# X by tokens through DRAM: VectorE turns squares and DMA reorders them, in place of TensorE's transposes

## Chip, cores and metric

One core of one Trainium2 chip runs the whole program. The metric is device microseconds of one execution, the median of several runs; lower is better.

## What is computed

Batch 4, 448 tokens, 12 heads of 64, so a model width of 768. An attention with sigmoid weights is followed by two token and channel blocks:

```python
x = sigmoid(q @ k.T / 8 - log(448)) @ v              # heads joined: (4, 448, 768)
u = x + (x.T @ U @ V).T                              # first block, tokens mixed at rank 32
x = u + relu(u @ w_ch1) @ w_ch2                      # 768 -> 3072 -> 768
theta = x @ w_theta                                  # second block: a rotation of x
zr, zi = x * cos(theta), x * sin(theta)
y = w_tok_r @ zr + w_tok_i @ zi                      # per batch, over tokens
u = x + y
out = u + relu(u @ w_ch)
```

## The kernel before

All of x stays on the chip as X, [128 partitions, 6, 1792]: feature d*128 + p on partition p of slab d, tokens of the four batches along the row. Nearly every product is done as three fp32r matmuls (high by high, high by low, low by high), so each operand is split in two parts, by ScalarE (high, `hi_act`) and by VectorE or GpSimd (low, `lo_dve`, `lo_pool`, lines 110 to 119).

The order of all instructions is written out by hand, engine by engine, in program order. The stages that matter here:

- **The channel block**, 12 blocks i of 256 hidden columns times 4 batches b. `ch1(i, b)` makes g in PSUM with 36 matmuls, ScalarE and VectorE split it (gh L671, gl L672), and `ch2(i, b)` runs a stage later: three tiles y (e2 = 0, 1, 2) of 12 matmuls each, from a ring of two PSUM buffers, each added to X by VectorE (L690). After each tile a function `after(e2)` does one or two steps of weight conversion (`tick`). So a y tile needs the buffer that the add of two tiles earlier frees. In the last block (i = 11, called L in the code) the order on TensorE is ch2(batch 0), ch1(batch 2), ch2(batch 1), ch1(batch 3), ch2(batch 2), ch2(batch 3).
- In that last block SyncE also loads tok (3.1 MB, the split token matrices) and three of the split w_theta slabs, and brings the last conversions in and out (`ws_wc`, `th_d`, `wc_d`).
- **The rotation**, 14 chunks of 128 tokens. `project(c)` makes theta for 128 tokens (36 matmuls, L799 to L803) in a ring of two PSUM tiles; `trig(c)` reduces it on VectorE (t1, L819 and L820, which frees the PSUM tile) and takes sine and cosine on ScalarE; `split_x(c + 2)` splits X for a later chunk; `zmake(c)` multiplies x by sine and cosine on VectorE (L854 and L856, or L864 and L865 for a chunk that lies in two batches) and splits the products (zh on ScalarE, zl mostly on GpSimd). Theta has tokens on partitions, X has features there, so `natural(c)` turns X first: six transposes of 128x128 on TensorE into PSUM (xn, L811). After chunks 4, 7 and 13 follow `mix(0)`, `mix(1)`, `mix(2)` and then `mix(3)`: six tiles of 21 matmuls each over the tokens of a batch, added to X by VectorE (L881) from two PSUM buffers. `zmake` of the chunk before stands inside `project(c)` on TensorE, after half of its matmuls, or inside a mix after its second tile.
- The tiles t1 and t2 come from rings of two, zr from a ring of two. A name in the profile is that of the tile, without its numbers.

All DMAs named here are issued by SyncE (SPq in the profile), one after another in program order, each when what it waits for has come.

Of the kernel before, what the change touches and what calls it, by code (L numbers as in the profile page):

```python
# [11 lines left out]
F32 = mybir.dt.float32  # L12
# [7 lines left out]
def f(t):  # L20
    return t.bitcast(F32)
# [3 lines left out]
def tile_kernel(  # L25
# [15 lines left out]
    nc = tc.nc  # L41
    B, H, S, D = q.shape
    DM = H * D
    R = moe_U.shape[1]
    DF = moe_w_ch1.shape[1]
    P = 128
    CP = 112
    NC = S // CP
    NK = DM // P
    NT = B * S  # L50
# [4 lines left out]
    HN = DM // 2  # L55
    NTC = NT // P
    REM = S % P
    NFULL = S // P
# [24 lines left out]
    cpool = ctx.enter_context(tc.tile_pool(name="cpool", bufs=1))  # L83
    wpool = ctx.enter_context(tc.tile_pool(name="wpool", bufs=1))

    dpool = ctx.enter_context(tc.tile_pool(name="dpool", bufs=1, space=bass.MemoryType.DRAM))

    ident = cpool.tile([P, P], F32, name="ident")
    bias_s = cpool.tile([P, 1], F32, name="bias_s")
    half_pi = cpool.tile([P, 1], F32, name="half_pi")  # L90
    X = cpool.tile([P, NK, NT], F32, name="X")
# [9 lines left out]
    def pool(name, side="left", space=None):  # L101
        st = ExitStack()
        kw = dict(name=name, bufs=1, side=side, reuse_waits="tile")
        if space is not None:
            kw["space"] = space
        return st.enter_context(tc.tile_pool(**kw)), st


    def hi_act(o, i):
        nc.scalar.activation(o, i, AF.Copy)  # L110
# [100 lines left out]

    kept = {}
    tok_d = dpool.tile([P, 2, NZ, S], F32, name="tok_d")

    def spill_tile(name):
        return late["sp"].tile([P, 2 * DM], F32, tag="sp", name=f"sp_{name}", bufs=1)
# [17 lines left out]
    def load_kept(name, tag):  # L234
        t = ring(tag, f"{name}_r")
        nc.sync.dma_start(out=f(t), in_=kept[name])
        return t
# [58 lines left out]
    late = {}  # L296
# [2 lines left out]
    ap, ap_st = pool("ap")  # L299
    ap1, ap1_st = pool("ap1")  # L300
    ap2, ap2_st = pool("ap2")
    ps_a, ps_a_st = pool("ps_a", "left", PSUM)
    ps_b, ps_b_st = pool("ps_b", "right", PSUM)
    u_in = ap.tile([P, 2, NS, R], F32, name="u_in")
# [167 lines left out]
    def U2(b, d, ps, hl, n=2):  # L472
        h, l = hl
        for m in range(n):
            nc.tensor.matmul(
                ps[:, m, :S], pc_t[b][:, (d + m) * P:(d + m + 1) * P], h, start=True, stop=False
            )
        for m in range(n):
            nc.tensor.matmul(
                ps[:, m, :S], pc_t[b][:2 * R, (d + m) * P:(d + m + 1) * P], l, start=False, stop=True  # L480
            )
        x = X[:, d:d + n, b * S:(b + 1) * S]
        nc.vector.tensor_add(x, ps[:, :n, :S], x)
# [28 lines left out]
    L = NB - 1  # L512
# [40 lines left out]
    def tick(i, b, t):  # L553
        for name in units.get((i, b, t), ()):
            plan[name].step()
# [26 lines left out]
    def split_u(b, p, d0, d1, *los):  # L582
        if d0 == 0:
            uh_t[b] = p.tile([P, NK, S], F32R, name=f"uh{b}")
            ul_t[b] = p.tile([P, NK, S], F32R, name=f"ul{b}")
        for d in range(d0, d1):
            x = X[:, d, b * S:(b + 1) * S]
            hi_act(uh_t[b][:, d], x)
            los[d % len(los)](ul_t[b][:, d], x, uh_t[b][:, d])
# [8 lines left out]
    for p in range(NP):  # L598
# [19 lines left out]
        b, r = divmod(p - 2 - NH, NH)  # L618
# [3 lines left out]
        b, r = divmod(p - 3 - NH, NH)  # L622
        if b >= 0 and r < NK // 2:
            ps = ps_a.tile([P, 2, 512], F32, tag="ux", name=f"h_{b}_{r}")
# [87 lines left out]

    u23, u23_st = pool("u23")
    ps_y, ps_y_st = pool("ps_y", "left", PSUM)
    def hook(i, b):
        def after(e2):
            if (i, b) == (0, 1):
                ps = ps_g.tile([P, FB, 512], F32, tag="g", name=f"hl_{e2}", bufs=2)
                U2(B - 1, 2 * e2, ps, (vhl, vll))
            if i == 0 and b in (1, 2):  # L720
                split_u(b + 1, u23, 2 * e2, 2 * e2 + 2, lo_pool)
            tick(i, b, e2 + 2)
        return after
# [15 lines left out]
    for i in range(NB):  # L739
        for b in range(B):  # L740
            tick(i, b, 0)
            if (i, b) not in ((0, 0), (0, 1)):
                ch1(i, b)
            if i == L and b == 1:
                u01_st.close()
                tokhl, tokhl_st = pool("tokhl", "right")
                ctx.enter_context(tokhl_st)
                tok = tokhl.tile([P, 2, NZ, S], F32R, name="tok")
                nc.sync.dma_start(out=f(tok), in_=tok_d)
                tok_h, tok_l = tok[:, 0], tok[:, 1]  # L750
                xr, xr_st = pool("xr", "right")
                ctx.enter_context(xr_st)
            if i == L and b >= 2:
                split_x(b - 2)
            if i == L and b == 0:
                th_t[0] = load_kept("th0", "w1")
            if i == L and b == B - 1:
                th_t[2] = load_kept("th2", "w1")
                th_t[3] = load_kept("th3", "w1")
            if i == L and b == 1:  # L760
                th_t[1] = load_kept("th1", "w2")
            tick(i, b, 1)
            if prev is not None:
                ch2(*prev, hook(i, b))
            prev = (i, b)
            if (i, b) == (0, 1):
                uv_st.close()
                late["sp"], sp_st = pool("sp")
# [2 lines left out]
    th_t[4] = load_kept("th4", "w2")  # L771
    th_t[5] = load_kept("th5", "w2")
    sp_st.close()
    u23_st.close()
    gpool_st.close()
    cv_st.close()
# [6 lines left out]
    ps_e, st = pool("ps_e", "left", PSUM)  # L783
    ctx.enter_context(st)
    zp, st = pool("zp")
# [3 lines left out]
    def project(c, w, name, k0=0, k1=NK):  # L789

        if k0 == 0:
            pj_t[c] = ps_t.tile([P, 2, 512], F32, tag="th", name=f"{name}_{c}", bufs=2)
        ps = pj_t[c]
        h, l = xs_t[c]
        for kk in range(k0, k1):
            wh, wl = w[kk][:, 0], w[kk][:, 1]
            for j in range(2):
                sl = slice(j * HN, (j + 1) * HN)
                nc.tensor.matmul(ps[:, j, :HN], h[:, kk, :], wh[:, sl], start=kk == 0, stop=False)  # L799
                nc.tensor.matmul(ps[:, j, :HN], h[:, kk, :], wl[:, sl], start=False, stop=False)  # L800
            for j in range(2):
                sl = slice(j * HN, (j + 1) * HN)
                nc.tensor.matmul(ps[:, j, :HN], l[:, kk, :], wh[:, sl], start=False, stop=kk == NK - 1)  # L803
        return ps[:, :, :HN]

    def natural(c, name):

        ps = ps_e.tile([P, 2, 512], F32, tag="xn", name=f"{name}_{c}")
        for kk in range(NK):
            j, o = divmod(kk * P, HN)  # L810
            nc.tensor.transpose(ps[:, j, o:o + P], X[:, kk, c * P:(c + 1) * P], ident)  # L811
        return ps[:, :, :HN]

    def trig(c):

# [10 lines left out]
    def zsplit(key, t, lo):  # L826
        h = zp.tile([P, 2, HN], F32R, tag="zh", name=f"zh_{key[0]}_{key[1]}", bufs=12)
        l = zp.tile([P, 2, HN], F32R, tag="zl", name=f"zl_{key[0]}_{key[1]}", bufs=12)
        hi_act(h, t)
        lo(l, t, h)  # L830
        z_t[key] = (h.rearrange("p a n -> p (a n)"), l.rearrange("p a n -> p (a n)"))

    def where(c):
        pr, ci = divmod(c, 2 * NFULL + 1)
        return pr, ci, 2 * pr + (ci > NFULL), ci if ci < NFULL else ci - NFULL - 1

    def zmul(c):
        cos, sin = T_t[c]
        xn = natural(c, "xn")
        nc.vector.tensor_mul(sin, xn, sin)  # L840
        nc.vector.tensor_mul(cos, xn, cos)

# [6 lines left out]
    def zmake(c):  # L849
        pr, ci, b, i = where(c)  # L850
        if ci != NFULL:
            cos, sin = T_t.pop(c)
            xn = natural(c, "xn")
            nc.vector.tensor_mul(sin, xn, sin)  # L854
            zsplit((b, NFULL + i), sin, lo_pool)
            nc.vector.tensor_mul(cos, xn, cos)  # L856
            zsplit((b, i), cos, lo_pool)
        else:
            cos, sin = T_t.pop(c)
            xn = natural(c, "xn")  # L860
            for n in range(2):
                t = zp.tile([P, 2, HN], F32, tag="zr", name=f"zr_{c}_{n}", bufs=2)
                sl = slice(n * REM, (n + 1) * REM)
                nc.vector.tensor_mul(t[REM:], xn[sl], sin[sl])  # L864
                nc.vector.tensor_mul(t[:REM], xn[sl], cos[sl])  # L865
                zsplit((2 * pr + n, 2 * NFULL), t, lo_pool if n else lo_dve)

    def mix(b, after=None):
        for d in range(NK):
# [12 lines left out]
            if after is not None:  # L882
                after(d)

    project(0, th_t, "th", 0, 4)
    project(1, th_t, "th", 0, 4)
    for c in range(NTC):
# [52 lines left out]
    for bi, b in enumerate(turns_):  # L940
        for e2 in range(NK // 2):
# [3 lines left out]
            else:  # L945
                ps = ps_t.tile([P, 2, 512], F32, tag="th", name=f"wc_{b}_{e2}", bufs=2)
# [3 lines left out]
            for e in range(2):  # L950
                m = 2 * e2 + e
                o = ps1[e][:, 0, :S] if final else ps[:, e, :S]
# [42 lines left out]
```

## Time and profile before

| | us |
|---|---|
| median of 3 runs (lowest, highest) | 1170.18 (1169.7, 1170.59) |
| the profiled execution | 1170.08 |
| its span, first to last instruction | 1168.3 |
| TensorE matmuls busy | 1155.3 |
| VectorE, ScalarE, GpSimd busy | 647.9, 360.9, 189.5 |
| last block of the channel block, ch2(batch 0) to the end of ch2(batch 3) | 830.9 to 875.2 |
| rotation, first project to the start of mix(3) | 875.2 to about 1053 |

The first two lines are times of whole executions; the rest is read from the trace of one of them, in us from its first instruction. A matmul's end is modelled and overlaps the next one, so a row's duration is longer than the step from one start to the next; that step is what a chain is made of. On VectorE, too, the next instruction starts about 0.1 us before the one ahead is over.

### The profile page before, as it was taken

How to read it: one execution, taken by the hardware profiler on the slowest of the kernel's cores; microseconds unless marked ns; L12 is line 12 of the kernel's file. 1: busy time of each engine (PE TensorE's matmuls, PEld its weight loads, DVE VectorE, ACT ScalarE, POOL GpSimd, SP SyncE). 2: the span in 40 equal slices, each digit the busy share in tenths (PEclk: the TensorE clock that was granted, in tenths of full speed). 3: DMA queues.
4: the chain of work that ended last, by engine and by line, in shares of the span. 5: the costliest groups of instructions: out<-in, count | busy, mean ns of one | idle time of the engine just before them, and what ended most of it. 6: DMA issues, size and time to landing. Idle time of an engine off the chain costs nothing.

```text
span 1168.3 us, 15638 instructions
## 1 busy us (share of the span) xinstructions
PE 1155.3 (99%) x6414; PEld 1000.5 (86%) x6414; DVE 647.9 (55%) x805; ACT 360.9 (31%) x465; POOL 189.5 (16%) x136
## 2 busy tenths in 40 slices
PE   7999999999999999999999999999999999999998
PEld 3444458999999999999999999999999999999997
DVE  4777873445554555455545556565375542732443
ACT  5878872212221222122212222222125341630110
POOL 2300012211111111111111122222002321410000
PEclk9999999999999999999999999999999999999999
DMA  9887830113231323132313242424431000120444
GB/s 168 165 162 141 161 83 1 55 54 97 51 133 54 97 52 131 54 97 53 130 54 98 66 140 61 155 61 156 164 138 52 1 1 1 45 119 1 61 64 66
DMA packets 183719, 100.57 MB, mean 86 GB/s; under 512 B 151232, under 2 KB 174656, under 8 KB 183520
## 3 DMA queue, kind: packets, MB, share of 16 engines
q1 hardware_dynamic: 156800, 87.95, 28.3%
q0 software_dynamic: 2368, 8.24, 2.5%
q10 hardware_dynamic: 24480, 3.39, 2.0%
q8 instruction: 50, 0.82, 0.3%
q14 instruction: 21, 0.17, 0.0%
HBM read 81.40 MB, written 18.15 MB: 85 GB/s over the span
## 4 chain that ended last, share of the span: by engine, by line
PE 97%; DMA 1%; SPq 1%; DVE 1%; ACT 0%; issue 0%; ACTq 0%
PE g L664 10%; PE g L666 10%; PE g L665 10%; PE y L686 10%; PE y L688 10%; PE y L687 10%; PE av L419 5%; PE sc L393 4%; PE y L877 3%; PE y L876 3%; PE y L878 3%; PE th L799 3%; PE th L803 3%; PE th L800 2%; PE wc L958 2%; PE wc L959 2%
## 5 line engine op out<-in xcount | busy, mean ns | idle before, releaser
L690 DVE TENSOR_TENSOR X<-y,X 128x896 f32<-128x896 f32 x144 | 157.1, 1091 | 114.9 <-PE y L688 113.5
L686 PE MATMUL y<-gh,w 128*128 128x448 f32 x576 | 210.7, 366 | 0.2 <-DVE X L690 0.2
L664 PE MATMUL g<-uh,w 128*128 128x448 f32 x576 | 210.7, 366 | 0.0
L687 PE MATMUL y<-gl,w 128*128 128x448 f32 x576 | 210.4, 365 | 0.0
L688 PE MATMUL y<-gh,w 128*128 128x448 f32 x576 | 210.4, 365 | 0.0
L666 PE MATMUL g<-uh,w 128*128 128x448 f32 x576 | 210.4, 365 | 0.0
L665 PE MATMUL g<-ul,w 128*128 128x448 f32 x576 | 210.4, 365 | 0.0
L671 ACT ACTIVATE gh<-g 128x896 fp32r<-128x896 f32 x48 | 44.1, 919 | 390.8 <-PE g L666 390.8
L672 DVE SCALAR_TENSOR_TENSOR gl<-g,gh 128x896 fp32r<-128x896 f32 x48 | 52.4, 1092 | 183.8 <-ACT gh L671 183.8
L113 POOL TENSOR_TENSOR w<-ca_w,w 128x768 fp32r<-128x768 f32 x42 | 77.8, 1853 | 432.0 <-ACT w L110 432.0
L664 PEld LDWEIGHTS g<-uh,w 128*128 128x128 f32 x576 | 108.2, 188 | 9.8 <-ACT uh L110 0.7
L686 PEld LDWEIGHTS y<-gh,w 128*128 128x128 f32 x576 | 108.2, 188 | 9.7 <-issue 1.1
L688 PEld LDWEIGHTS y<-gh,w 128*128 128x128 f32 x576 | 108.2, 188 | 8.6
L666 PEld LDWEIGHTS g<-uh,w 128*128 128x128 f32 x576 | 108.2, 188 | 8.6
L687 PEld LDWEIGHTS y<-gl,w 128*128 128x128 f32 x576 | 108.2, 188 | 8.6
L665 PEld LDWEIGHTS g<-ul,w 128*128 128x128 f32 x576 | 108.2, 188 | 8.5
L384 ACT ACTIVATE A<-sc,bias_s 128x896 f32<-128x896 f32 x72 | 72.2, 1006 | 23.4 <-PE sc L393 12.8
L419 PE MATMUL av<-A,v 128*64 128x448 f32 x288 | 65.2, 561 | 0.0
L876 PE MATMUL y<-tok,zh 128*128 128x448 f32 x168 | 61.7, 367 | 0.0
L877 PE MATMUL y<-tok,zh 128*128 128x448 f32 x168 | 61.5, 366 | 0.0
L113 POOL TENSOR_TENSOR zl<-t,zh 128x768 fp32r<-128x768 f32 x23 | 42.7, 1880 | 115.4 <-ACT zh L110 115.4
L878 PE MATMUL y<-tok,zl 128*128 128x448 f32 x168 | 61.4, 366 | 0.0
(139 smaller groups left out, 1634.6 us busy)
## 6 DMA issues: line engine op xcount, KB each, us to landing
ws_w<-in_moe_w_ch_dram SPq DMA_DIRECT2D x40, 768.0 KB, 4.4
ws_w<-in_moe_w_ch_dram POOLq DMA_DIRECT2D x8, 768.0 KB, 5.9
k<-in_k_dram SPq DMA_DIRECT2D x94, 56.0 KB, 2.7
q<-in_q_dram SPq DMA_DIRECT2D x93, 56.0 KB, 3.1
ws_th<-in_moe_w_theta_dram SPq DMA_DIRECT2D x6, 768.0 KB, 4.3
th_d<-sp_th SPq DMA_DIRECT2D x6, 768.0 KB, 4.1
ws_wc<-in_moe_w_ch_dram SPq DMA_DIRECT2D x6, 768.0 KB, 4.7
wc_d<-sp_wc SPq DMA_DIRECT2D x6, 768.0 KB, 4.5
```

The lines of the kernel that those rows point to most:

```text
L113: nc.gpsimd.tensor_sub(o, a, b)
L419: nc.tensor.matmul(ps[h * D:(h + 1) * D, :S], v_t[p // 2][:, 2 * (p % 2) + h, c, :], A_t[p, c][:, h, :], start=c == 0 and p % 2 == 0, stop ...
L664: nc.tensor.matmul(o, wh[:, sl], uh_t[b][:, kk, :], start=kk == 0, stop=False)
L665: nc.tensor.matmul(o, wh[:, sl], ul_t[b][:, kk, :], start=False, stop=False)
L666: nc.tensor.matmul(o, wl[:, sl], uh_t[b][:, kk, :], start=False, stop=kk == NK - 1)
L686: nc.tensor.matmul(o, wh[:, sl], gh[:, j, :], start=j == 0, stop=False)
L687: nc.tensor.matmul(o, wh[:, sl], gl[:, j, :], start=False, stop=False)
L688: nc.tensor.matmul(o, wl[:, sl], gh[:, j, :], start=False, stop=j == FB - 1)
L690: nc.vector.tensor_add(x, ps[:, :, :S], x)
L876: nc.tensor.matmul(o, zh[:, sl], tok_h[:, i, :], start=n == 0, stop=False)
L877: nc.tensor.matmul(o, zh[:, sl], tok_l[:, i, :], start=False, stop=False)
L878: nc.tensor.matmul(o, zl[:, sl], tok_h[:, i, :], start=False, stop=n == NZ - 1)
```

## The change

X by tokens is no longer made by TensorE. VectorE turns X in squares of 32x32 (one instruction for a slab of 448 tokens, `turn_x`), SyncE writes the turned slab to DRAM (x_d), and later reads a chunk back so that tokens lie on partitions (`load_xn`: four DMAs of 32 partitions by 24 pieces of 32 numbers, 128 bytes each). The turns of batches 0, 1 and 2 stand in `after` of the last block, two behind each add, through a ring of three staging tiles; those of batch 3 stand behind the channel block and use buffers of t1 and t2. xn is now a tile in SBUF, from the ring zr, which has three buffers instead of two. The tile `ident` moves to another pool; it is now only used by the first transposes of the program.

```diff
+    x_d = dpool.tile([DM, NT], F32, name="x_d")
...
+    def turn_x(b, d, t):
+        nc.vector.transpose(out=t, in_=X[:, d, b * S:(b + 1) * S])
+        nc.sync.dma_start(out=x_d[d * P:(d + 1) * P, b * S:(b + 1) * S], in_=t)
+
     def hook(i, b):
         def after(e2):
+            if i == L and 0 < b < B:
+                for d in (2 * e2, 2 * e2 + 1):
+                    turn_x(b - 1, d, late["stg"].tile([P, S], F32, tag="stg", name=f"stg_{b}_{d}", bufs=3))
...
-    def natural(c, name):
-
-        ps = ps_e.tile([P, 2, 512], F32, tag="xn", name=f"{name}_{c}")
-        for kk in range(NK):
-            j, o = divmod(kk * P, HN)
-            nc.tensor.transpose(ps[:, j, o:o + P], X[:, kk, c * P:(c + 1) * P], ident)
-        return ps[:, :, :HN]
+    xn_t = {}
+
+    def load_xn(c):
+        t = xn_t[c] = zp.tile([P, 2, HN], F32, tag="zr", name=f"xn_{c}", bufs=3)
+        for a in range(P // R):
+            o = c * P + a * R
+            nc.sync.dma_start(
+                out=t[a * R:(a + 1) * R].rearrange("i a (g j) -> i (a g) j", j=R),
+                in_=x_d[:, o:o + R].rearrange("(g i) j -> i g j", i=R),
+            )
...
-            xn = natural(c, "xn")
+            xn = xn_t.pop(c)
...
+            load_xn(c + 1)
+        _, second, _, _ = where(c + 1)
+        if c + 2 < NTC and second != NFULL:
+            load_xn(c + 2)
...
+    load_xn(0)
+    load_xn(1)
+    for d in range(NK):
+        tag = f"t{d % 2 + 1}"
+        t = zp.tile([P, 2, HN], F32, tag=tag, name=f"stg_{B}_{d}", bufs=2).rearrange("p a n -> p (a n)")[:, :S]
+        turn_x(B - 1, d, t)
     project(0, th_t, "th", 0, 4)
     project(1, th_t, "th", 0, 4)
```

On VectorE, from the second add of batch 0 to the second add of batch 1 in the last block, there stood (L690 is the add of a y tile, L672 makes gl, L119 makes xl, the others convert w_theta; in brackets what an instruction waits for, DMAHW being a DMA's landing):

```order
L690 TENSOR_TENSOR X<-y_0_1_6653,X 128x2x448 [waits PE_49]
L151 SCALAR_TENSOR_TENSOR ws_th_6389<-ca_th_6636,ws_th_6389 128x768 [waits DVE_49,Activation_49]
L690 TENSOR_TENSOR X<-y_0_2_6668,X 128x2x448 [waits PE_49]
L157 SCALAR_TENSOR_TENSOR ca_th_6636<-ca_th_6636,ws_th_6389 128x768 [waits DVE_49,Pool_49]
L672 SCALAR_TENSOR_TENSOR gl_2_6721<-g_2_6683,gh_2_6720 128x896 [waits Activation_49]
L119 TENSOR_TENSOR xl_0_6725<-X,xh_0_6724 128x768 [waits Activation_49]
L690 TENSOR_TENSOR X<-y_1_0_6730,X 128x2x448 [waits PE_49]
```

and the same place of the changed kernel (lines are one higher or lower there; stg is a staging tile, L717 its turn):

```order
L691 TENSOR_TENSOR X<-y_0_1_6663,X 128x2x448 [waits PE_49]
L717 STREAM_TRANSPOSE stg_2_6677<-X 128x448 [waits DVE_49]
L717 STREAM_TRANSPOSE stg_3_6680<-X 128x448 [waits DMAHW5_49]
L150 SCALAR_TENSOR_TENSOR ws_th_6390<-ca_th_6640,ws_th_6390 128x768 [waits Activation_49]
L691 TENSOR_TENSOR X<-y_0_2_6684,X 128x2x448 [waits PE_49]
L717 STREAM_TRANSPOSE stg_4_6698<-X 128x448 [waits DMAHW6_49,DVE_49]
L717 STREAM_TRANSPOSE stg_5_6701<-X 128x448 [waits DMAHW7_49]
L156 SCALAR_TENSOR_TENSOR ca_th_6640<-ca_th_6640,ws_th_6390 128x768 [waits Pool_49]
L673 SCALAR_TENSOR_TENSOR gl_2_6743<-g_2_6705,gh_2_6742 128x896 [waits Activation_49]
L118 TENSOR_TENSOR xl_0_6747<-X,xh_0_6746 128x768 [waits Activation_49]
L691 TENSOR_TENSOR X<-y_1_0_6752,X 128x2x448 [waits PE_49]
```

Two turns now stand behind each add, and from the fourth on each waits for the landing of the write that frees its staging tile.

On SyncE, at the step from the channel block to the rotation, there stood the last spills, the last two loads of w_theta, and then only the loads of w_ch (wc), which come 140 us later:

```order
L231 DMA th_d<-sp_th_6846 128x1536 [waits DMAHW0_49,DVE_49,Activation_49]
L231 DMA wc_d<-sp_wc_6897 128x1536 [waits DMAHW1_49,Pool_49]
L236 DMA th_r<-th_d 128x1536 [waits DMAHW5_49,DMAHW2_49,PE_49]
L236 DMA th_r<-th_d 128x1536 [waits DMAHW3_49,DMAHW0_49,PE_49]
L236 DMA wc_r<-wc_d 128x1536 [waits DMAHW4_49,PE_49]
```

and now, behind the same two loads, the reads of chunks 0 and 1 and then the writes of batch 3:

```order
L236 DMA th_r<-th_d 128x1536 [waits DMAHW5_49,DMAHW0_49,PE_49]
L822 DMA xn_7008<-x_d 32x24x32 [waits DMAHW6_49]
L822 DMA xn_7008<-x_d 32x24x32 [waits DMAHW7_49]
L822 DMA xn_7008<-x_d 32x24x32
L822 DMA xn_7008<-x_d 32x24x32 [waits DMAHW1_49]
L822 DMA xn_7013<-x_d 32x24x32 [waits DMAHW2_49,DVE_49]
L822 DMA xn_7013<-x_d 32x24x32 [waits DMAHW3_49]
L822 DMA xn_7013<-x_d 32x24x32 [waits DMAHW4_49]
L822 DMA xn_7013<-x_d 32x24x32 [waits DMAHW5_49]
L718 DMA x_d<-stg_0_7018 128x448 [waits DMAHW6_49,DVE_49]
L718 DMA x_d<-stg_1_7021 128x448 [waits DMAHW7_49,DVE_49]
L718 DMA x_d<-stg_2_7024 128x448 [waits DMAHW0_49,DVE_49]
```

Eight reads stand between the loads of w_theta and the first write of batch 3; a DMA also waits for the landing of the eighth DMA ahead of it. On VectorE the fifth turn of batch 3 waits for the landing of that batch's first write, and the first instruction of trig(0) stands behind the sixth.

## Rows read from the trace of the kernel before

**Rows 1.** The page, busy time by engine.
```profile
PE 1155.3 (99%) x6414; PEld 1000.5 (86%) x6414; DVE 647.9 (55%) x805; ACT 360.9 (31%) x465; POOL 189.5 (16%) x136
```

**Rows 2.** Timeline of TensorE, five places: start us, us, what [idle before, releaser].
```profile
845.44 0.36 PE L686 MATMUL y<-gh,w 128*128 128x448 f32 x1
...
852.74 0.36 PE L664 MATMUL g<-uh,w 128*128 128x448 f32 x1
...
867.68 0.44 PE L686 MATMUL y<-gh,w 128*128 128x448 f32 x1 [0.20 <-DVE X L690]
...
875.20 0.34 PE L799 MATMUL th<-th_r,xh 128*128 128x384 f32 x1
...
918.17 0.81 PE L811 MATMUL xn<-ident,X 128*128 128x128 f32 x6
```

**Rows 3.** Timeline of VectorE in the last block.
```profile
854.67 0.95 DVE L157 SCALAR_TENSOR_TENSOR ca_th<-ca_th,ws_th 128x768 uint32<-128x768 uint32 x1
...
861.24 1.09 DVE L672 SCALAR_TENSOR_TENSOR gl<-g,gh 128x896 fp32r<-128x896 f32 x1 [5.63 <-ACT gh L671]
862.25 0.95 DVE L119 TENSOR_TENSOR xl<-X,xh 128x768 fp32r<-128x768 f32 x1
863.12 1.08 DVE L690 TENSOR_TENSOR X<-y,X 128x896 f32<-128x896 f32 x1
...
866.46 1.08 DVE L690 TENSOR_TENSOR X<-y,X 128x896 f32<-128x896 f32 x1
```

**Rows 4.** Timeline of VectorE at the start of the rotation.
```profile
885.80 0.96 DVE L819 TENSOR_SCALAR t<-th 128x768 f32<-128x768 f32 x1 [9.31 <-PE th L803]
...
895.94 0.96 DVE L854 TENSOR_TENSOR t<-xn,t 128x768 f32<-128x768 f32 x1 [2.00 <-PE xn L811]
...
900.16 2.52 DVE L119 TENSOR_TENSOR xl<-X,xh 128x768 fp32r<-128x768 f32 x1
...
917.50 0.61 DVE L881 TENSOR_TENSOR X<-y,X 128x448 f32<-128x448 f32 x1
```

**Rows 5.** The chain that ended last, 889 to 893 us: start, us, what.
```profile
891.04 0.35 PE th L803 x2
891.39 0.66 PE xn L811 x6
```

**Rows 6.** VectorE groups by form: busy us, mean ns of one, idle before.
```profile
L440 DVE STREAM_TRANSPOSE xT<-X 128x448 f32<-128x448 f32 x24 | 15.2, 637 | 0.1
```

**Rows 7.** Timeline of SyncE, two issues: start us, us of the issue.
```profile
831.97 0.35 SPq L194 DMA_DIRECT2D ws_wc<-in_moe_w_ch_dram  x1
...
873.20 0.32 SPq L231 DMA_DIRECT2D wc_d<-sp_wc  x1
```

**Rows 8.** DMA issues at 831.04, 831.97 and 875.4: KB, us from issue to landing.
```profile
tok<-tok_d SPq DMA_DIRECT2D x1, 3136.0 KB, 10.3
...
ws_wc<-in_moe_w_ch_dram SPq DMA_DIRECT2D x1, 768.0 KB, 13.1
...
th_r<-th_d SPq DMA_DIRECT2D x1, 768.0 KB, 5.7
```

**Rows 9.** Timeline of TensorE near 26 us.
```profile
26.16 0.59 PE L402 MATMUL sl<-qT,kT 64*64 64x448 f32 x2 [1.77 <-DVE qT L354]
```

**Rows 10.** Windows: stretch, busy us by engine (instructions), granted clock, DMA share, GB/s.
```profile
27.20:30.60 3.40, 3.40 (x14) 1.85 (x14) 3.07 (x7) 1.88 (x3) 0.55 (x2) 0.50 0.66 108
```

**Rows 11.** DMA queues, 1086 to 1092 us (pieces of 128 bytes): packets, MB, share.
```profile
q10 hardware_dynamic: 1503, 0.18, 22.8%
q1 hardware_dynamic: 1377, 0.17, 19.0%
```

**Rows 12.** DMA queues, 303 to 307.6 us (loads of 256-byte pieces).
```profile
q1 hardware_dynamic: 1856, 0.46, 44.5%
```

**Rows 13.** Timeline of GpSimd there.
```profile
894.61 7.25 POOL L113 TENSOR_TENSOR zl<-t,zh 128x768 fp32r<-128x768 f32 x4 [21.44 <-ACT zh L110]
```

More of the change, by code (lines that the diff above doesn't have):

```diff
@@ L86, in tile_kernel @@
     dpool = ctx.enter_context(tc.tile_pool(name="dpool", bufs=1, space=bass.MemoryType.DRAM))
-    ident = cpool.tile([P, P], F32, name="ident")
     bias_s = cpool.tile([P, 1], F32, name="bias_s")
@@ L301, in tile_kernel @@
     ap2, ap2_st = pool("ap2")
+    ident = ap2.tile([P, P], F32, name="ident")
     ps_a, ps_a_st = pool("ps_a", "left", PSUM)
@@ L752, in tile_kernel @@
                 ctx.enter_context(xr_st)
+                late["stg"], stg_st = pool("stg", "right")
             if i == L and b >= 2:
@@ L773, in tile_kernel @@
     sp_st.close()
+    stg_st.close()
     u23_st.close()
@@ L852, in zmake @@
             cos, sin = T_t.pop(c)
-            xn = natural(c, "xn")
+            xn = xn_t.pop(c)
             nc.vector.tensor_mul(sin, xn, sin)
@@ L859, in zmake @@
             cos, sin = T_t.pop(c)
-            xn = natural(c, "xn")
+            xn = xn_t.pop(c)
             for n in range(2):
-                t = zp.tile([P, 2, HN], F32, tag="zr", name=f"zr_{c}_{n}", bufs=2)
+                t = zp.tile([P, 2, HN], F32, tag="zr", name=f"zr_{c}_{n}", bufs=3)
                 sl = slice(n * REM, (n + 1) * REM)
```

## The prediction

> **What bounds the kernel now.** The page's busy times come first: TensorE is busy 1155.3 of 1168.3 us, the others at most 55% [rows 1]. The waits of TensorE say whether that is real: past the first 30 us it waits once, for 0.2 us, in the last block of the channel block, before the row at 867.68 [rows 2]. So a microsecond that leaves TensorE's stream is worth a microsecond, as long as no other engine is then late. Which one is near to late is read stage by stage. The timelines of VectorE show two places without room: the last tiles of the last block (an unbroken run from 861.24 to past 866.46, at whose end TensorE waits [rows 2, 3]) and the start of the rotation. There VectorE works from 885.80 to the first add of mix(0) at 917.50 [rows 4], and that add ends at 918.11, 0.06 us before TensorE has finished its second mix tile and starts the next transposes at 918.17 [rows 2]. The third mix tile needs the buffer that this add frees. Without the transposes it would start at 918.17 at once: from 885.8 to 918 VectorE, not TensorE, is what a faster TensorE would run into.
>
> The profiled execution took 1170.08 us, 1.8 more than its span and 0.1 less than the median; the sum is made against it. Faster or slower means by over 0.2% (2.3 us), about what a measurement of this kernel can tell.
>
> **What is removed.** Six transposes take 0.66 us of the chain [rows 5], and there are 14 chunks: 9.3 us at most. Four groups (chunks 0 to 3) stand before the add at 918 that ends last, ten after it: 10 x 0.66 = 6.6 us that I count, 2.7 that I don't.
>
> **Turns in the last block.** A turn of a 448-token slab is like L440's, 0.64 us [rows 6], or 0.57 from start to start; a pair costs VectorE 1.13. The first three go into staging tiles at once. The fourth waits for the first write. That write is issued at about 835, behind tok, a w_theta load and ws_wc. Issued within 1 us, tok lands at 841.4 and ws_wc, a quarter of its size, only at 845.1 (831.97 + 13.1) [rows 7, 8]: one queue, in order, and 768 KB take about 1.9 us of it, so 224 KB take 0.55 (an estimate from these landings). The first write then lands at 845.6, and VectorE stands from about 837.8 to there. TensorE doesn't mind at first: ch1(2) runs until 845.44 [rows 2]. Then:
>
> - VectorE still owes the fourth turn (0.57), a conversion step (0.95 long, 0.87 as a step, like xl to X [rows 3]) and the third add of batch 0 (1.09): done at 848.1. TensorE, at 2.43 us a tile (7.30 for three, 845.44 to 852.74 [rows 2]), wants that buffer at 847.9: it waits 0.4.
> - Then two turns 1.13, conversion 0.87, gl 1.01, xl 0.87, first add of batch 1 1.09: 853.0. TensorE has finished its second tile at 850.7 and waits 2.3 for that add.
> - ch2(2) starts 2.7 late. Before, from gl's start at 861.24 to the end of the second add were 6.3 us and TensorE began its next tile 0.35 late [rows 2, 3]. With two turns in between it is 7.4, so TensorE waits 1.1 more. For each of the next two adds VectorE needs 1.13 + 0.87 + 1.00 = 3.0 against 2.43: 0.56 each.
>
> Together **+5.0**. Bounds: if writes land at once, the first two waits vanish and 2.2 stay, since the pairs themselves cost that in the run after 861; if the write to DRAM takes 1 us longer to be confirmed, 6.
>
> **The clock.** TensorE idled 1.8 us before L402 at 26.16 [rows 9]; in the stretch that followed its granted clock was 0.50, so 1.2 GHz in place of 2.4, for the 3.4 us of [rows 10]. Two of the waits forecast here are longer (2.3 us, and about 4 at the boundary). I expect the same stretch after each: 1.7 us of TensorE's work lost. After the first nothing covers it, **+1.7** (bounds 0 and 3.4); after the second TensorE runs ahead of a VectorE that is later still, so it costs nothing.
>
> **The boundary.** Count from T, the first project (875.20 before [rows 2]). The last w_theta load was issued at 875.4 and landed 5.7 later, T + 5.9 [rows 8]. The spill wc_d, issued at 873.20, 2.0 before T [rows 7], now goes out just before T, as the step that feeds it stands behind the turns; its 1.9 us of queue push the load to about T + 7.0. Behind it are eight reads of 768 pieces of 128 bytes. The output's pieces of that size show the price: (22.8% + 19.0%) x 16 engines x 6 us / 2880 packets = 13.9 ns a packet [rows 11], so 0.67 us a read and 5.4 for eight: T + 12.4. The first write of batch 3 stands behind them, T + 13.0. VectorE's fifth turn waits for it, the sixth follows, and trig(0) starts at T + 14.2. Before it was T + 10.6 (885.80 [rows 4]), and project(2), which needs its PSUM tile at T + 12.5 (72 matmuls at 0.174, as in [rows 5]), got it just in time. So **+3.6**. Bounds: reads limited only by issue at 0.5 us each, +2.3; the dearest strided loads that the trace has, 44.5% x 16 x 4.6 us / 1856 = 17.6 ns a packet [rows 12], +5.1. The later reads (chunk 2 on) are asked for one to two chunks ahead, 6 us each, and take 2.7 plus landing: hidden.
>
> **From there to mix(0).** VectorE took 31.7 us from trig(0) to the add at 917.50 [rows 4]. It loses the 2.0 that it waited for the transposes (the row at 895.94). But its multiplications read xn from SBUF now, where they read PSUM. In the trace xl, which reads X and xh in SBUF, took 2.52 us at 900.16 in place of 0.95, done 0.8 after GpSimd's run of four subtractions ended at 901.86, while L854 at 895.94, one operand from PSUM, took 0.96 in the midst of that run [rows 3, 4, 13]. So multiplications that meet a subtraction (1.8 us each [rows 13]) will wait. Laying the order out with these durations, two do, cosine of chunk 1 and the first one of chunk 3: 1.8 each; the tile t1 for chunk 2 is freed 1.3 later by the same subtractions; 1.0 of waiting for ScalarE goes. Net -2.0 + 1.8 + 1.3 + 1.8 - 1.0 = **+1.9**, between -2.0 (no such waits) and +5 (two more). The Trainium skill, SBUF - State Buffer, section "Who interferes with whom", says it as a rule: a VectorE instruction with two SBUF inputs shuts out, and is shut out by, a GpSimd instruction that reads SBUF, for the whole instruction. The two rows agree with it. By the rule the sum below stands; if only xl's kind were hit, it would be 3.9 lower.
>
> The add that frees mix(0)'s third tile is then 5.0 + 1.7 + 3.6 + 1.9 = 12.2 late. Behind it VectorE has room, so the ten groups that are left come off in full; I take 0.5 for small waits of the same kind around chunks 7 and 13.
>
> **The sum.** 1170.1 + 12.2 - 6.6 + 0.5 = **1176.2 us**, slower by 0.5%.
>
> **Rivals.**
>
> - *The writes don't queue.* If small writes land some 3 us after issue whatever is ahead of them (the output's pieces take 2.6 when nothing is), the waits of VectorE for staging tiles go, and with them 2.8 of the last block, the clock's 1.7 and the boundary's 3.6: 1176.2 - 8.1 = 1168.1; if multiplications don't meet subtractions either, 3.9 less, 1164.2. With every turn hidden it is 1170.1 - 9.3 = 1160.8. It decides where the first write of batch 0 lands: before about 839 there is no wait. For it: 16 engines serve the queue, and a packet of 1792 bytes is small. Against: three loads of [rows 8] landed strictly one behind the other.
> - *The same time.* The clock stays up in the last block and half of the meetings on VectorE fail: 1176.2 - 1.7 - 1.9 = 1172.6; with reads at 0.5 us as well, 1171.3.
> - *Slower still.* Reads of 128 bytes from rows 7 KB apart cost more than the output's pieces. At 17.6 ns it is +1.4, at twice the price +5.4 at the boundary; past 1 us a read the later chunks' reads come late too. 1178 to 1184.
>
> **Chances.** The sum as it stands 0.55, writes that don't queue 0.15 (two thirds of it below 1167.7), the same time 0.15, slower still 0.15. The likeliest one's own range is 1173 to 1180. Eight in ten: 1168 to 1181.5. Faster 0.11, same 0.14, slower 0.75.
>
> **What would show it.** The turn stg after the second add of batch 0 should sit idle some 8 us for a DMA and end that wait near 845.7; TensorE should wait about 2.3 us for an add in ch2(1) and have a stretch at half clock behind it; the fifth turn of batch 3 should wait about 9 us for a DMA, and project(2) about 4 us for VectorE's second step on chunk 0; multiplications should show durations near 2.8 in place of 0.95; from mix(0)'s third tile on, chunks should be 0.66 us shorter each. Wrong would be: writes landing within 3 us, no waits of TensorE in ch2(1), or later reads that hold up `zmake`.

## The result: 1182.13 us, slower by 1.0%

The changed kernel takes 1182.13 us (median of 5, 1181.56 to 1183.35) against 1170.18 of the kernel before on the same chip: ratio 1.0104, 95% interval 1.0092 to 1.0115, 11.95 us more. Forecast were +6.0 us and a range up to 1181.5. The sign was right, and so were the places where VectorE was to be late; the size was not, and nearly half of the gap lies in a place to which the forecast gave nothing.

The page of after, busy time by engine (answers to [rows 1]), and TensorE's waits from the last block on (total us, times, longest):

```profile
PE 1153.2 (98%) x6330; PEld 993.3 (84%) x6330; DVE 666.9 (57%) x829; ACT 360.5 (31%) x465; POOL 190.0 (16%) x136
```

```profile
PE y L687 <- DVE X L691: 5.9, 5, 2.2
PE th L809 <- DVE t L833: 5.1, 1, 5.1
...
PE th L813 <- DVE xl L118: 1.4, 2, 1.0
PE y L893 <- DVE X L898: 1.4, 1, 1.4
```

84 transposes are gone (6414 to 6330 matmuls), which by [rows 5] were worth 9.3 us, but TensorE's busy time fell by only 2.1, and it now waits some 14 us, all for VectorE. Six pairs of rows show where the 11.9 us between the two spans were added. TensorE's first matmul of the rotation in after, T in what follows:

```profile
882.30 0.33 PE L809 MATMUL th<-th_r,xh 128*128 128x384 f32 x1
```

VectorE's timeline of after, the same places as in [rows 3, 4] and three more (L673 and L672 make gl, L832 is trig(0), L898 and L881 the adds of a mix, L947 and L924 the adds of the last product):

```profile
832.52 1.09 DVE L673 SCALAR_TENSOR_TENSOR gl<-g,gh 128x896 fp32r<-128x896 f32 x1 [7.21 <-ACT gh L672]
...
847.66 0.65 DVE L717 STREAM_TRANSPOSE stg<-X 128x448 f32<-128x448 f32 x1 [9.29 <-DMA x_d<-stg]
...
896.81 1.20 DVE L717 STREAM_TRANSPOSE stg<-X 128x448 f32<-128x448 f32 x2 [11.08 <-DMA x_d<-stg]
897.94 0.96 DVE L832 TENSOR_SCALAR t<-th 128x768 f32<-128x768 f32 x1
...
904.71 0.96 DVE L118 TENSOR_TENSOR xl<-X,xh 128x768 fp32r<-128x768 f32 x1 [2.10 <-ACT xh L109]
...
908.19 2.61 DVE L869 TENSOR_TENSOR t<-xn,t 128x768 f32<-128x768 f32 x1
912.54 0.96 DVE L832 TENSOR_SCALAR t<-th 128x768 f32<-128x768 f32 x1 [1.74 <-POOL zl L112]
...
921.51 2.45 DVE L877 TENSOR_TENSOR zr<-xn,t 64x768 f32<-64x768 f32 x1
...
932.32 1.14 DVE L898 TENSOR_TENSOR X<-y,X 128x448 f32<-128x448 f32 x2
...
1041.88 0.62 DVE L898 TENSOR_TENSOR X<-y,X 128x448 f32<-128x448 f32 x1 [1.29 <-PE y L895]
...
1115.04 1.09 DVE L947 SCALAR_TENSOR_TENSOR X<-wc,X 128x896 f32<-128x896 f32 x1 [1.47 <-PE wc L982]
...
1122.48 1.09 DVE L947 SCALAR_TENSOR_TENSOR X<-wc,X 128x896 f32<-128x896 f32 x1 [1.34 <-PE wc L982]
...
1174.55 0.62 DVE L947 SCALAR_TENSOR_TENSOR X<-wcl,X 128x448 f32<-128x448 f32 x1 [2.41 <-PE wcl L982]
```

Rows of VectorE in before that [rows 3, 4] do not hold:

```profile
832.06 1.09 DVE L672 SCALAR_TENSOR_TENSOR gl<-g,gh 128x896 fp32r<-128x896 f32 x1 [7.21 <-ACT gh L671]
...
1032.52 0.62 DVE L881 TENSOR_TENSOR X<-y,X 128x448 f32<-128x448 f32 x1 [2.37 <-PE y L878]
...
1104.27 1.09 DVE L924 SCALAR_TENSOR_TENSOR X<-wc,X 128x896 f32<-128x896 f32 x1 [1.33 <-PE wc L959]
1111.56 1.09 DVE L924 SCALAR_TENSOR_TENSOR X<-wc,X 128x896 f32<-128x896 f32 x1 [1.26 <-PE wc L959]
...
1162.64 0.62 DVE L924 SCALAR_TENSOR_TENSOR X<-wcl,X 128x448 f32<-128x448 f32 x1 [2.34 <-PE wcl L959]
```

| up to | before | after | later by | added since the line above | forecast |
|---|---|---|---|---|---|
| gl of the last block's start | 832.06 | 832.52 | 0.46 | 0.46 | 0 |
| first project, T | 875.20 [rows 2] | 882.30 | 7.10 | 6.64 | 5.0 + 1.7 |
| trig(0) | 885.80 [rows 4] | 897.94 | 12.14 | 5.04 | 3.6 |
| first add of mix(0) | 917.50 [rows 4] | 932.32 | 14.82 | 2.68 | 1.9 |
| second add of mix(2) | 1032.52 | 1041.88 | 9.36 | -5.46 | -6.6 + 0.5 |
| last add | 1162.64 | 1174.55 | 11.91 | 2.55 | 0 |

The first line is no effect of the change: the kernels below, all alike up to there but for tok's load, stand between 0.5 us earlier and 2.1 later at that place. The last line is the surprise. From the second add of mix(2) to the last one nothing is changed, TensorE waits for nothing in either trace, and the clock is granted in full; yet a tile of the last product, 36 matmuls, takes 7.44 us (1115.04 to 1122.48) in place of 7.29 (1104.27 to 1111.56). TensorE steps from one 448-column matmul to the next in 206.7 ns where it stepped in 202.7.

### The profile page after: what moved, and what is told of

It reads as the page before. It is cut to its first block, busy times and chain, and to the rows that moved or that the text cites. A ratio compares the mean times of both kernels' runs of the same rounds, so it can differ in the third digit from the quotient of the medians.

```text
span 1180.2 us, 15632 instructions
## 1 busy us (share of the span) xinstructions
PE 1153.2 (98%) x6330; PEld 993.3 (84%) x6330; DVE 666.9 (57%) x829; ACT 360.5 (31%) x465; POOL 190.0 (16%) x136
## 4 chain that ended last, share of the span: by engine, by line
PE 86%; DVE 5%; DMA 4%; SPq 2%; issue 1%; ACT 1%; POOL 0%; ACTq 0%; DVEq 0%
PE g L665 10%; PE g L667 10%; PE g L666 10%; PE y L687 9%; PE y L689 9%; PE y L688 9%; PE av L420 4%; PE sc L394 3%; PE y L893 3%; PE y L894 3%; PE y L895 3%; PE wc L981 2%; PE wc L982 2%; PE wc L980 2%; DMA q<-in_q_dram 2%; DMA x_d<-stg 1%
## 5 line engine op out<-in xcount | busy, mean ns | idle before, releaser
L672 ACT ACTIVATE gh<-g 128x896 fp32r<-128x896 f32 x48 | 44.1, 919 | 391.4 <-PE g L667 391.4
L673 DVE SCALAR_TENSOR_TENSOR gl<-g,gh 128x896 fp32r<-128x896 f32 x48 | 52.4, 1092 | 173.3 <-ACT gh L672 173.3
L893 PE MATMUL y<-tok,zh 128*128 128x448 f32 x168 | 61.8, 368 | 1.4 <-DVE X L898 1.4
L809 PE MATMUL th<-th_r,xh 128*128 128x384 f32 x168 | 57.4, 342 | 5.1 <-DVE t L833 5.1
```

What stands on the lines that cost most here:

```text
L893: nc.tensor.matmul(o, zh[:, sl], tok_h[:, i, :], start=n == 0, stop=False)
```

## Experiments

Each was timed against the kernel before, on the same chip, 4 to 11 runs each; on the four chips of these runs the kernel before took 1170.4 to 1170.8 us. Differences from the changed kernel are given between medians; by the ratios they come out 0.4 to 0.8 us larger.

| kernel | median us | ratio to before (95%) | expected us |
|---|---|---|---|
| b1_transposes_ahead | 1174.95 | 1.0038 (1.0025 to 1.0050) | 1172.8 |
| a1b_one_short | 1179.32 | 1.0074 (1.0061 to 1.0087) | 1179.6 |
| a2_tok_late | 1177.59 | 1.0062 (1.0049 to 1.0074) | 1177.7 |
| a3_writes_first | 1176.66 | 1.0054 (1.0040 to 1.0068) | 1177.1 |
| a6_six_buffers | 1175.06 | 1.0038 (1.0024 to 1.0052) | 1175.8 |
| a4_from_psum | 1181.30 | 1.0090 (1.0075 to 1.0105) | 1179 |
| a5_filled | 1182.11 | 1.0097 (1.0080 to 1.0114) | 1182.1 |
| b2_no_transposes | 1167.25 | 0.9970 (0.9959 to 0.9981) | 1164.0 |
| c1_all_three | 1170.87 | 1.0007 (0.9998 to 1.0016) | 1169.6 |
| c3_all_four | 1169.17 | 0.9989 (0.9981 to 0.9998) | 1168.6 |
| c2_late_chunks | 1166.53 | 0.9968 (0.9957 to 0.9979) | 1166.2 |

### The step of TensorE: b1_transposes_ahead and a1b_one_short

In the trace of before the step is 206.7 ns through the first tile of mix(2) and 202.7 after the six transposes that stand behind it; in after, with no transposes, it stays at 206.7 to the end. The first kernel takes the transposes out of mix(2) of the kernel before:

```diff
+        if c == NTC - 1:
+            project(c, th_t, "th", k0, NK - 1)
+            xn_last = natural(c, "xn")
+            k0 = NK - 1
         project(c, th_t, "th", k0, NK)
```

> The kernel before, with the six transposes of chunk 13 taken out of mix(2) and put ahead of the last 6 matmuls of 384 columns of project(13). Same work. In the trace of after, TensorE steps from one 448-column matmul to the next in 206.7 ns from mix(2) to the end of the program; in the trace of before it does so only until the six transposes after the first tile of mix(2), and from there in 202.7 ns on average. Theory (the transposes bring the short step back): here nothing brings it back, so 663 matmuls (5 tiles of mix(2), all of mix(3), 432 of the last product) take 4.0 ns more each: 1170.2 + 2.65 = 1172.8 us. Rival (the step has another cause than the transposes): 1170.2 us, the short step in the last product.

Two steps from tile to tile in the last product (VectorE's timeline):

```profile
1107.69 1.09 DVE L928 SCALAR_TENSOR_TENSOR X<-wc,X 128x896 f32<-128x896 f32 x1 [1.47 <-PE wc L963]
1115.13 1.09 DVE L928 SCALAR_TENSOR_TENSOR X<-wc,X 128x896 f32<-128x896 f32 x1 [1.41 <-PE wc L963]
```

7.44 us, as in after. From the second add of mix(2) (1034.53) to the last one (1167.21) it is 132.68 us against 130.12 before, so +2.56 for 2.65 expected. The time is some 4.4 us above before by the ratio; most of the rest is a wait that the edit itself made (TensorE for the buffer of the transposes):

```profile
PE xn L811 <- DVE t L856: 1.6, 1, 1.6
```

The second kernel adds one short matmul to the changed kernel, at the place where the transposes stood:

```diff
+    def after_mix2(d):
+        if d == 0:
+            ps = ps_e.tile([P, 2, 512], F32, tag="xn", name="short")
+            nc.tensor.matmul(ps[:, 0, :P], z_t[2, 0][0][:, :P], tok_h[:, 0, :P], start=True, stop=True)
+            zmul(NTC - 1)
+    mix(2, after_mix2)
```

> The changed kernel with one matmul of 128 columns more, after the first tile of mix(2); its product is used by nothing. Theory (any stumble in the stream of matmuls brings TensorE from the 206.7 ns step to the 202.7 ns step, transposes were only one): the last product steps in 202.7 ns, 663 x 4.0 ns = 2.65 less, 0.1 to 0.2 for the matmul: 1182.1 - 2.5 = 1179.6 us. Rival (it takes transposes, or another cause): 1182.2 us, with 206.7 ns to the end.

```profile
1106.20 1.09 DVE L952 SCALAR_TENSOR_TENSOR X<-wc,X 128x896 f32<-128x896 f32 x1 [1.31 <-PE wc L987]
1113.50 1.09 DVE L952 SCALAR_TENSOR_TENSOR X<-wc,X 128x896 f32<-128x896 f32 x1 [1.33 <-PE wc L987]
```

7.30 us a tile, and 1179.32, 2.8 below the changed kernel. One matmul more makes 663 others faster. So transposes are not needed for the short step behind mix(2)'s first tile: a short matmul there does as well. All traces agree: the five kernels with one or the other at that place step in 202.7 ns to the end, the eight without in 206.7.

In mix(0) and mix(1) the step doesn't hang on the transposes. In mix(1) the ten kernels without transposes there all go over to 202.7 within the first tile, after a single step of 218 to 231 ns, for which no wait is recorded. In mix(0) TensorE waits before the third tile, and the same wait left it at the long step in after and at the short one in a6_six_buffers; TensorE's wait and two adds of VectorE behind it, in after and then in a6:

```profile
932.98 0.47 PE L893 MATMUL y<-tok,zh 128*128 128x448 f32 x1 [1.39 <-DVE X L898]
```

```profile
941.97 0.62 DVE L898 TENSOR_TENSOR X<-y,X 128x448 f32<-128x448 f32 x1 [3.72 <-PE y L895]
946.31 0.62 DVE L898 TENSOR_TENSOR X<-y,X 128x448 f32<-128x448 f32 x1 [3.71 <-PE y L895]
```

```profile
926.37 0.47 PE L893 MATMUL y<-tok,zh 128*128 128x448 f32 x1 [1.39 <-DVE X L898]
```

```profile
935.19 0.62 DVE L898 TENSOR_TENSOR X<-y,X 128x448 f32<-128x448 f32 x1 [3.63 <-PE y L895]
939.44 0.62 DVE L898 TENSOR_TENSOR X<-y,X 128x448 f32<-128x448 f32 x1 [3.63 <-PE y L895]
```

A tile of 21 matmuls takes 4.34 us in the one and 4.25 in the other. Why TensorE keeps to one step or the other, and which of the two a disturbance leaves it in, no run here tells.

### The last block: a2_tok_late

```diff
-                nc.sync.dma_start(out=f(tok), in_=tok_d)
...
+    nc.sync.dma_start(out=f(tok), in_=tok_d)
     project(0, th_t, "th", 0, 4)
```

> The changed kernel with the 3.1 MB load of tok issued behind the writes of batch 3 at the start of the rotation, and not ahead of the writes of batch 0. Theory (in the last block the writes stand behind tok): the first write lands near 838 in place of 847.6, VectorE waits no more than 1 us for a staging tile, the last block loses 2.2 us in place of 6.65, and the time is 1182.1 - 4.4 = 1177.7 us. Rival (the pairs of turns themselves, or writes that are slow whatever stands ahead, delay the adds): 1181 us or more, with TensorE's waits in the last block as before.

In the changed kernel the queue was as forecast, and dearer. DMA issues at 831.50 to 835.74 of after (KB, us to landing; answers to [rows 8]):

```profile
tok<-tok_d SPq DMA_DIRECT2D x1, 3136.0 KB, 10.5
th_r<-th_d SPq DMA_DIRECT2D x1, 768.0 KB, 12.0
ws_wc<-in_moe_w_ch_dram SPq DMA_DIRECT2D x1, 768.0 KB, 14.6
```

```profile
x_d<-stg SPq DMA_DIRECT2D x1, 224.0 KB, 11.9
```

ws_wc lands 3.1 us after th_r (832.43 + 14.6 against 831.87 + 12.0) where 1.9 were priced, with the first write behind it; that write lands at 847.64, 1.6 after the forecast's 845.6 when the 0.46 is taken off. With tok out of the way the first write lands 1.9 us after its issue, at 838.1, and no turn waits; TensorE's waits in that block are

```profile
PE y L687 <- DVE X L691: 2.0, 3, 1.4
```

T is 2.2 us later than before (878.27, less 0.87 at the block's start and 875.20):

```profile
878.27 0.34 PE L808 MATMUL th<-th_r,xh 128*128 128x384 f32 x1
```

That is what the pairs of turns cost by themselves, 2.2 in the forecast too. The writes cost the other 4.4, and the time falls by 4.5.

### The boundary: a3_writes_first and a6_six_buffers

The first puts the writes ahead of the reads, the second leaves the order and gives each turn of batch 3 a buffer of its own:

```diff
-    load_xn(0)
-    load_xn(1)
     for d in range(NK):
...
         turn_x(B - 1, d, t)
+    load_xn(0)
+    load_xn(1)
```

```diff
-        tag = f"t{d % 2 + 1}"
-        t = zp.tile([P, 2, HN], F32, tag=tag, name=f"stg_{B}_{d}", bufs=2).rearrange("p a n -> p (a n)")[:, :S]
+        t = f(zp.tile([P, 2, HN], F32R, tag="zh", name=f"stg_{B}_{d}", bufs=12)).rearrange("p a n -> p (a n)")[:, :S]
```

> The changed kernel with the turns and writes of batch 3 ahead of the eight reads of chunks 0 and 1 at the start of the rotation. Theory (the reads hold up the writes for which VectorE's fifth turn waits): the turn's wait falls from 11.1 to about 5 us, trig(0) starts when project(0) is done, 5.0 us earlier against the project, the stretch at half clock there goes, and the time is 1182.1 - 5.0 = 1177.1 us. Rival (the reads of chunks 0 and 1 come too late then, or the stretch from trig(0) to mix(0) is set by GpSimd and ScalarE): 1180 us or more.

> The changed kernel with batch 3's turns staged in six of the twelve buffers of zh, which are empty then, and not in t1 and t2. No turn there waits for a write, and the first sine no longer writes a buffer that a DMA still reads. Theory: both the boundary's 5.05 us go (trig(0) starts 10.6 us after the first project, as before the change), and 1.3 us behind it: in the trace of after ScalarE's table load of 1.28 us starts only when VectorE's second step on chunk 0 is done, and VectorE then waits 2.1 us for xh; before the change the table load ran earlier and that wait was 0.77. 1182.1 - 6.35 = 1175.8 us. Rival (the late table load has another cause): 1177.1 us, the wait for xh stays 2.1 us.

The first, VectorE's timeline:

```profile
892.59 1.19 DVE L717 STREAM_TRANSPOSE stg<-X 128x448 f32<-128x448 f32 x2 [7.31 <-DMA x_d<-stg]
893.72 0.96 DVE L832 TENSOR_SCALAR t<-th 128x768 f32<-128x768 f32 x1
```

The wait is 7.3 and not 5, since the last w_theta load lands at 891.91, 10.0 after T (881.86), even without reads behind it. Still trig(0) comes at T + 11.9, where it came at T + 15.6, and the time falls by 5.5. The half clock that was to go with the wait came all the same, at 912 to 916 us. In the second no turn waits, trig(0) is at T + 10.6 (892.66, T 882.06) as before the change, and the stretch behind it shortens as well. VectorE there, and ScalarE ahead of it:

```profile
898.12 0.96 DVE L118 TENSOR_TENSOR xl<-X,xh 128x768 fp32r<-128x768 f32 x1 [0.78 <-ACT xh L109]
```

```profile
893.19 1.28 ACT L834 ACT_TABLE_LOAD   x1
```

In the trace of after the same table load stands behind VectorE's second step on chunk 0, and xl waits 2.10 (904.71 above); in before it ran ahead of it and xl waited 0.77:

```profile
899.95 1.28 ACT L834 ACT_TABLE_LOAD   x1 [6.52 <-DVE t L833]
```

The order of ScalarE's instructions with their waits, before and after, says why: the first sine had to wait for the landing of a write out of its buffer too, and two of its waits, that one among them, moved to the table load ahead of it.

```
L821 ACT_TABLE_LOAD
L821 ACTIVATE t_0_7015<-t_0_7014 128x768 [waits DVE_49]
...
L834 ACT_TABLE_LOAD [waits DMAHW1_49,DVE_49]
L834 ACTIVATE t_0_7102<-t_0_7101 128x768 [waits Pool_49]
```

From trig(0) to mix(0)'s first add it is 33.0 us here (892.66 to 925.70) against 34.4 in after and 31.7 before. The time falls by 7.1, where 6.35 were expected, with runs that scatter by 1 us.

### VectorE's port: a4_from_psum

```diff
-            xn = xn_t.pop(c)
+            xn = (xn_t.pop(c), xn_ps)[1]
...
+    xn_ps = ps_e.tile([P, 2, 512], F32, tag="xn", name="xn_ps")[:, :, :HN]
+    nc.scalar.activation(xn_ps, X[:, 0:2, :HN], AF.Copy)
```

> The changed kernel, all turns, writes and reads kept, but the products with sine and cosine read a PSUM tile that ScalarE fills once (so the output isn't the reference's). Theory (a multiplication with two SBUF operands waits while GpSimd subtracts): the two of 2.61 and 2.45 us at 908.19 and 921.51 in the trace of after fall to about 0.95, the first add of mix(0) comes 3 us earlier against trig(0), and the time is 1182.1 - 3 = 1179 us. Rival (they were long for another reason, or what waits behind them waits for GpSimd anyway): 1182 us.

```profile
908.21 0.95 DVE L869 TENSOR_TENSOR t<-xn_ps,t 128x768 f32<-128x768 f32 x1
911.80 0.96 DVE L832 TENSOR_SCALAR t<-th 128x768 f32<-128x768 f32 x1 [2.65 <-POOL zl L112]
...
921.03 0.95 DVE L877 TENSOR_TENSOR zr<-xn_ps,t 64x768 f32<-64x768 f32 x1 [0.36 <-ACT t L834]
922.95 0.95 DVE L878 TENSOR_TENSOR zr<-xn_ps,t 64x768 f32<-64x768 f32 x1 [0.96 <-ACT t L836]
```

Both multiplications fall from 2.6 and 2.45 to 0.95 us with one operand out of PSUM, in the midst of the same subtractions. The Trainium skill, SBUF - State Buffer, section "Who interferes with whom", has this as a rule, and here the trace agrees. But of the 3.1 us only 1.05 come back by the first add of mix(0) (33.3 us from trig(0) in place of 34.4): the next step on chunk 2 then waits 2.65 for GpSimd in place of 1.74, and the two products of chunk 3 wait 1.3 for ScalarE. The time, 1181.3, is 0.8 below the changed kernel, less than its scatter (1178.77 to 1182.19). The expected 3 us had left out what stood right behind.

### The clock: a5_filled

In after the granted clock falls behind the wait of 5.06 us, for twice the time of [rows 10], and nowhere in the last block (windows: stretch, busy us by engine, clock, DMA share, GB/s):

```profile
898.77:905.59 6.82, 5.56 (x17) 5.59 (x18) 4.66 (x7) 5.53 (x7) 0.00 (x0) 0.50 0.49 100
```

```diff
+        if c == 2:
+            ps = ps_e.tile([P, 2, 512], F32, tag="xn", name="fill")
+            for m in range(20):
+                nc.tensor.matmul(ps[:, m % 2, :S], th_t[0][:, 0, :P], tok_h[:, 0, :], start=True, stop=True)
```

> The changed kernel with 20 matmuls of 448 columns ahead of project(2), where TensorE waits 5.1 us for trig(0); nothing uses their product. They take 4.1 us of the wait, so that TensorE is not idle there. Theory of the prediction (the half clock behind that wait costs nothing, since VectorE is later still): the stretch at half clock goes and the time stays at 1182.1 us. Rival (VectorE waits for ScalarE's xh, which waits for matmuls at half clock): the 3.4 us that TensorE lost in 6.8 us at half clock come back in part, 1180 us or less.

```profile
897.00:904.00 7.00, 6.35 (x35) 5.75 (x34) 4.82 (x7) 4.90 (x6) 0.00 (x0) 1.00 0.55 122
915.30:922.12 6.82, 6.11 (x19) 6.11 (x20) 6.69 (x7) 5.87 (x8) 4.33 (x2) 0.50 0.00 1
```

The half clock didn't go, it came 16 us later, still ahead of the first add, so the whole time says little. What the run does tell: with project(2) at full clock VectorE still waits 2.1 for xh, and still takes 34.3 us from trig(0) to the first add. A kernel that keeps the full clock all through that stretch is a6:

```profile
890.00:926.00 36.00, 33.11 (x178) 30.73 (x176) 29.58 (x27) 23.72 (x29) 14.25 (x7) 1.00 0.49 96
```

Its 33.0 us from trig(0) to the first add are the 34.4 of after less the table load's 1.33, which leaves nothing for the clock. So behind the boundary wait the half clock cost VectorE nothing, as forecast.

### The most that could be gained: b2_no_transposes

> The kernel before without any of the 84 transposes of the rotation, and without turns, writes and reads: the products with sine and cosine read one PSUM tile, which ScalarE fills once (it leaves X by tokens out, so the output isn't the reference's). It is the most that the change could gain. Theory (without transposes the step of 206.7 ns stays): 14 x 0.66 = 9.3 less, about 690 matmuls x 4.0 ns = 2.8 and some 0.3 in mix(0) and mix(1) more: 1170.2 - 6.2 = 1164.0 us. Rival (the step of the last product has another cause): 1160.9 us.

It takes 3.1 us off, not 9.3 and not 6.2. VectorE's first add of mix(0) stands at 917.07, only 0.15 earlier when the 0.29 at this run's start is taken off: the four groups ahead of it bring nothing, as [rows 4] let expect and as the expectation forgot. From there to the second add of mix(2) (1026.24 against 1032.52) 5.85 us come off, of 6.6 for the ten groups; 0.41 of the rest is a wait of TensorE for VectorE in project(13). Behind it the step is 206.7 ns and takes 2.6 back. In sum the trace is 3.7 us shorter; this profiled run was the fastest of seven.

### All repairs, and a better place: c1_all_three, c3_all_four, c2_late_chunks

c1 joins the edits of a2, a3 and a1b; c3 those of a2, a6 and a1b.

> The changed kernel with the three repairs at once: tok's load behind the rotation's first reads, batch 3's writes ahead of those reads, one short matmul in mix(2). If the three causes are separate, their sizes add: 1182.1 - 4.5 (tok, as measured) - 5.5 (writes first, as measured) - 2.5 (short step) = 1169.6 us. Rival (they delay the same add before mix(0), where GpSimd and ScalarE then set the time): 1172 us or more.

> The changed kernel with tok's load late, batch 3 staged in zh, and one short matmul in mix(2): all 14 chunks through DRAM, with no wait that the staging or the queue makes. If the terms add: 1170.9 (the three repairs, measured) less the 0.95 us that trig(0) was still late there and 1.3 us of the table load: 1168.6 us. Rival (what is left is VectorE's turns and its port, and both stay): 1170.5 us or more. Either way it should not beat 1167.25 us, the time measured with no transposes and no turns, by more than the 2.6 us of the short step.

1170.87 and 1169.17: the causes add up to within 1.3 and 0.6 us. With each wait that the queue and the staging made taken away, and the short step brought back by the added matmul, c3 has what is left of the change, a gain of 0.1% (0.02% to 0.19%).

c2 goes the other way: it keeps TensorE's transposes where VectorE has no room, and turns batches 1 to 3 behind the adds of mix(0) and mix(1):

```diff
+            def after0(d):
+                if d == 1:
+                    zmake(c)
+                if 2 <= d <= 4:
+                    stage(1, (2 * d - 4, 2 * d - 3))
+                if d == 4:
+                    load_xn(5)
+                    load_xn(6)
+            mix(0, after0)
```

> The kernel before with only chunks 5, 6, 8, 9, 11 and 12 through DRAM. The turns of batch 1 stand in mix(0) and those of batches 2 and 3 in mix(1), where VectorE is busy about 40% and the rings t1 and t2 are free for staging; the other eight chunks keep TensorE's transposes, so each mix keeps one group inside it. Theory (the last block and the first chunks have no room, the mixes have): 6 x 0.66 = 4.0 less, nothing else: 1166.2 us, faster than both kernels. Rival (turns between the adds of a mix, or reads that come late, hold TensorE up): 1169 us or more.

```profile
924.61 1.16 DVE L717 STREAM_TRANSPOSE stg<-X 128x448 f32<-128x448 f32 x2
928.32 0.62 DVE L912 TENSOR_TENSOR X<-y,X 128x448 f32<-128x448 f32 x1 [2.55 <-PE y L909]
```

A pair of turns lies in a gap that still leaves VectorE 2.55 us idle before the next add; no turn and no multiplication waits for a DMA. From the last block on TensorE waits once, for the 0.2 us of before, and mix(2) keeps its transposes, so the last product steps in 202.7 ns. 1166.53 us, within 0.4 of what was expected, is 0.32% below the kernel before (0.21% to 0.43%), the best of all here.

## Why the prediction was wrong

- **The step that failed is "Behind it VectorE has room, so the ten groups that are left come off in full".** VectorE did have room, but the transposes were priced at their own 0.66 us, and the matmuls around them were taken, without a reason, to keep their duration. They didn't: from mix(2)'s second tile to the end they step in 206.7 ns in place of 202.7, which cost 2.55 us (shown by b1 and a1b, both ways). The trace of before hinted at it: in each mix the matmuls step in 206.7 ns ahead of the transposes and in 202.7 behind them. No row of the prediction looked at TensorE's step.
- **Last block, +6.7 forecast, 6.64 measured: right by luck, two errors that cancel.** The pairs cost 2.2, as forecast, but the writes 4.4 (2.8), as ws_wc landed later than in its turn: TensorE's first wait was 1.70 in place of 0.4. The half clock (+1.7) didn't come: waits of 1.70 and 2.21 us passed at full clock.
- **Boundary, +3.6 forecast, 5.04 measured**, at the upper bound of 5.1. The reads were right: they land 0.6 us apart (0.67), eight of them 5.0 us. The mis-sized term is the last w_theta load, T + 9.0 and not T + 7.0: it lands 3.2 us behind the load ahead of it, not 1.9. Reads are not what slows it (a3, 4.3 behind with writes after it); what does stays open.
- **Stretch to mix(0), +1.9 forecast, 2.68 measured.** Its named terms came: the two multiplications (2.61 and 2.45), the later t1 (a wait of 1.74 for GpSimd, 0.53 before), the vanished wait for transposes, the vanished waits for ScalarE. Missing was the table load, 1.33, since a wait for a staging write was put on it (a6). The price of the two multiplications overstates what their removal gives: 1.05 of 3.1 (a4).
- **What came off, -6.1 forecast, -5.46 measured.** Of the ten groups' 6.6 us 1.14 were lost, where 0.5 was allowed: 0.26 to the long step in mix(0), where the distance to before grows from 14.35 to 14.61 us over its last tiles, and 0.44 to a wait for VectorE's xl in project(13). The rest is not traced. The 0.26 can't be put down to the missing transposes, since a6 lacks them too and steps short there.
- **Rivals.** *The writes don't queue* is refuted by the 11.9 us to landing above. Its ceiling of 1160.8 was too low by 6.4 (b2). *Slower still* has the measured time in its 1178 to 1184, but by luck: the reads were cheaper than priced, not dearer.

In sum 5.8 us were missed: 2.55 of step, 1.44 at the boundary, 0.78 in the stretch, 0.64 less given back, 0.46 of scatter at the start, and -0.06 in the last block.

## What to carry to other kernels

Before work is taken off an engine, look at how the work around it runs with it and without it: here six transposes also set the pace of 663 matmuls, and a single short matmul in their place did the same. Place turns, staging and their DMAs in a stage where the helping engine has idle gaps before each step and the queue is empty; turns and DMAs that lost time in the last block and at the boundary lost none in the mixes (c2). Where a buffer is lent to a DMA, follow who uses it next: its wait can move to an earlier instruction and hold up an engine that had nothing to do with it.

## What the runs showed of the hardware

- TensorE has two steady steps for the same 448-column matmul at full clock, 206.7 and 202.7 ns. It can keep one for hundreds of matmuls. In mix(2) six transposes or one 128-column matmul turned the long step into the short one; in mix(0) a wait of 1.39 us was followed by the long step in after and by the short one in a6.
- The granted clock doesn't follow a wait's length alone: behind 1.77 us at 26 us of before it fell to half [rows 9, 10], behind 2.21 in the last block of after it stayed at 1.00 (0.50 and 1.00 are 1.2 and 2.4 GHz).
- A load of 768 KB with small DMAs right behind it landed 3.1 us (ws_wc) and 3.2 us (the last w_theta load, 4.3 in a3) after the load ahead of it, where the same loads came 1.9 to 2.0 us apart in before.
- ScalarE's table load takes 1.28 us, and it can carry the waits of the activation behind it, so that it no longer runs ahead (1.33 us in after).
- VectorE's multiplication with both operands in SBUF took 2.45 and 2.61 us beside GpSimd's subtractions, and 0.95 with one operand in PSUM (a4).
